# Two loads of a state-space and MLP kernel change places: the second piece of b1 and the broadcast of b2

## The chip, the cores and the metric

The kernel runs on one core of one Trainium2 chip. The core has TensorE (matmuls into PSUM, 8 banks), VectorE, ScalarE and GpSimd, which compute side by side, and SyncE (SP), which here only issues DMAs. ScalarE can issue DMAs too. The metric is the device time of one execution in microseconds. Before the change it is 149.21 us, the median of 3 runs (149.14 to 149.53).

## What is computed

The input x has 2048 rows of 448 columns (bf16). A layer norm gives xn. One branch is a diagonal state-space layer over the 2048 rows, the other a small MLP on a second layer norm of xn; the result is `x + s * silu(mlp)`:

```python
def reference(x, ..., w1, b1, w2, b2):            # cut to what matters
    xn = layernorm(x)
    # state space: 448 complex states, one recurrence over the rows
    Bu = xn @ B_bar.T                              # B_bar from Lambda, dt, B
    h[t] = Lam_bar * h[t - 1] + Bu[t]
    s = 2 * (h @ C.T).real + xn * Dskip
    # MLP, 448 -> 1792 -> 448
    y = layernorm(xn)
    g = gelu_tanh(y @ w1 + b1) @ w2 + b2
    return x + s * silu(g)
```

b1 has 1792 values, b2 has 448. Both are small; what matters here is when they arrive and what their loads stand in front of.

## The kernel before

**Groups.** The rows are worked in four groups of 512 rows (`NG = 4`), each of two blocks. Per group: both layer norms, the transposes of the normalized rows, the matmuls with B (`bu`, line 657), the recurrence as scans on VectorE (`ssm`, line 681), the first MLP layer (`mm1`, line 723), the second (`mm2`, line 748), and the output matmuls with C (`ym`, line 768).

**The order is written out by hand.** Every step is a task with the keys that it reads and writes; `emit` (line 131) walks the list `ORDER` (line 206), and each engine gets its tasks in that order. An engine runs its list strictly in order: where a task waits, all that stands behind it on that engine waits too. A number in `ORDER` is the place of a task among those without a name, in the order in which the program makes them; a name (`H000`, `T1`, `U03`) is a named TensorE task. The PSUM bank of every result is written out as well (`BANKS`); a task that takes over a bank waits for all tasks that used it before.

The numbers that matter here:

- 11 to 13: the loads of x, blocks 0 and 1 (lines 387 to 389); 37: x of blocks 2 and 3 (line 405)
- 14, 15: the two halves (k = 0, 1) of the first chunk of w1; 21 to 26: the halves of chunks 1, 2 and 3 (`ldw1`, line 382). All go through SP's queue.
- 16 to 18, then 19 and 20: loads that ScalarE issues. 19 is the first piece of b1 (two of its 14 columns of 128, line 393), 20 the second (the other twelve, line 394): 128 partitions with three runs of 4 values each, so 384 runs of 8 bytes.
- 35: b2 copied to all 128 partitions (`b2bc`, line 403), 128 times the same 896 bytes, on SP's queue. Its first reader is the head of `mm2` (line 754), which puts b2 into the PSUM banks of the second layer.
- 38: `b1f`, b1 from bf16 to f32, on ScalarE (line 527). It needs both pieces of b1. Every GELU uses it as its bias.
- 78, 83, 88: ScalarE's copies of the transposed first group out of PSUM (line 458).
- 96, 100, ...: the GELUs of the first layer (line 741 for half tiles, line 729 for whole ones).

**The first group.** Its first three pairs of w1's columns are done in two halves of rows (`mm1_half`, line 733: `H000`, `H010`, `H020`, `H011`, ...), so that work can begin when the first blocks are there. Each half pair takes two PSUM banks, so four of them fill all eight; the next one needs a GELU to have drained its banks. Before `H000` TensorE runs matmuls on a tile of zeros (line 809), which compute nothing.

**What else the steps of the prediction touch.** The cosines and sines of the recurrence are made once (`tables`, line 588): VectorE's steps at lines 591 to 596, then the sine on ScalarE (line 602), behind a table load (line 348) that follows the last GELU of the first group, and VectorE's negative copy of it (line 604). VectorE's list has the statistics of the second group's rows (line 430) ahead of these steps. The matrix B comes by transposing DMAs on SP (line 399); VectorE copies its last columns (line 626) and clears a part (line 627) before `bu` can use them at line 668.

Of the kernel before, what the change touches and what calls it, by code (L numbers as in the profile page):

```python
# [203 lines left out]


ORDER = [int(k) if k.isdigit() else k for k in """
18 17 16 4 11 12 13 14 2 3 ST I0 I4 0 35 10 1 I1 I2 I6 74 75 76 19 79 80 81 77 84 82 85 7 15 89 90 T0 78 I5 86 21 T2 I3 87 20 9 91 94 92 83
I7 H000 PV T1 39 6 41 8 40 88 T3 42 93 117 38 22 23 H010 95 44 H020 99 H011 103 96 H021 100 101 24 25 26 37 224 222 226 34 144 228 31 H04 32
104 102 105 223 118 5 54 55 H05 109 45 43 33 123 47 106 122 H001 227 115 225 229 46 111 48 110 112 124 314 49 230 97 H06 98 H03 113 193 107
56 121 125 198 DH 28 202 30 50 53 52 63 116 60 126 127 129 114 108 131 128 132 134 58 59 61 64 65 120 199 200 119 27 203 318 312 316 234 235  # L210
206 204 207 311 315 241 237 205 231 57 62 67 69 130 232 36 313 317 29 70 194 208 195 209 196 135 238 136 145 166 197 236 137 233 U00 167 66
# [670 lines left out]
```

## Time and profile before

| | before |
|---|---|
| median of 3 runs | 149.21 us |
| the profiled execution | 149.81 us |
| its span, first to last instruction | 147.8 us |
| TensorE busy, share of the span | 141.7 us, 96% |
| VectorE | 128.1 us, 87% |
| ScalarE | 103.6 us, 70% |
| GpSimd | 42.0 us, 28% |
| moved by DMA | 14.08 MB |

The profile is one execution. Its times count from the start of the span. "PE" is TensorE, "PEld" its weight loads, "DVE" VectorE, "ACT" ScalarE, "POOL" GpSimd, and a q behind an engine's name is its instruction queue, where DMAs are issued; L741 is line 741 of the program. A row of the timeline gives start, length, engine, line, operation, what it writes and reads, its size and how many instructions are merged in it; in square brackets stands how long the engine was idle before and what ended that. The chain that ended last is followed back from the last instruction, at each step to what released it. "To landing" is the time from the issue of a DMA until all of it has arrived.

### The profile page before, as it was taken

The page shows a single profiled execution, that of the slowest core. Times are in us where ns is not written, and L with a number is a line of the kernel's source. Part 1 is how long each engine was busy: PE and PEld are TensorE (multiplying, and loading weights), DVE is VectorE, ACT ScalarE, POOL GpSimd, SP SyncE. Part 2 cuts the span into 40 slices and gives each one's busy share as a digit, 9 for nine tenths or more (in the row PEclk, how much of TensorE's full clock was granted, in tenths as well). Part 3 has the DMA queues.
Part 4 walks back from the last instruction along what each step waited for, and adds up shares of the span by engine and source line. Part 5 has one row for each costly group of instructions (what it writes and reads, how often), then busy time and mean ns, then how long its engine had stood idle before and what let it go on. Part 6 is the DMA issues. An engine that isn't in the chain of part 4 may idle for free.

```text
span 147.8 us, 2863 instructions
## 1 busy us (share of the span) xinstructions
PE 141.7 (96%) x1092; PEld 72.8 (49%) x1092; DVE 128.1 (87%) x182; ACT 103.6 (70%) x148; POOL 42.0 (28%) x88
## 2 busy tenths in 40 slices
PE   6984999999999999999999999999999999999993
PEld 1573644554454434555553544554435455555563
DVE  2942992597499999989999998999999999999994
ACT  3225999989989989999988999924996610090300
POOL 2589397630000499760000005000009500000000
PEclk9999999999999999999999999999999999999999
DMA  4699997699793300100254601035003300003033
GB/s 105 187 352 347 368 178 146 108 244 155 127 161 61 75 0 4 36 0 18 45 114 103 122 1 42 0 59 101 4 0 98 98 0 7 0 0 98 0 124 124
DMA packets 32083, 14.08 MB, mean 95 GB/s; under 512 B 24131, under 2 KB 31686, under 8 KB 32070
## 3 DMA queue, kind: packets, MB, share of 16 engines
q1 hardware_dynamic: 31376, 13.83, 40.7%
q8 instruction: 8, 0.13, 0.4%
q10 hardware_dynamic: 694, 0.07, 0.4%
q14 instruction: 5, 0.04, 0.1%
HBM read 5.63 MB, written 1.84 MB: 50 GB/s over the span
## 4 chain that ended last, share of the span: by engine, by line
PE 91%; DMA 4%; DVE 2%; ACT 1%; issue 0%; ACTq 0%
PE psum L648 40%; PE psum L762 29%; PE psum L780 14%; DMA b1b<-in_B_b_dram 4%; PE psum L809 3%; PE psum L668 2%; PE psum L783 2%; PE psum L754 1%; DVE t L786 1%; DVE tmp L790 1%; ACT gT L741 1%; PE psum L455 0%; ACT b1f L527 0%; DVE still L339 0%; ACTq L158 0%
## 5 line engine op out<-in xcount | busy, mean ns | idle before, releaser
L648 PE MATMUL psum<-xn2T,w_sb 64*128 64x512 bf16 (+1 forms) x434 | 44.9, 356 | 2.5 <-ACT gT L741 2.1
L762 PE MATMUL psum<-w_sb,gT 128*128 128x448 bf16 x224 | 43.7, 353 | 0.0
L729 ACT ACTIVATE gT<-psum,b1f 128x512 bf16<-128x512 f32 x50 | 30.8, 696 | 5.6 <-PE psum L648 5.6
L648 PEld LDWEIGHTS psum<-xn2T,w_sb 64*128 64x128 bf16 x434 | 23.3, 108 | 21.8 <-ACT gT L741 2.3
L762 PEld LDWEIGHTS psum<-w_sb,gT 128*128 128x128 bf16 x224 | 21.7, 98 | 21.3 <-issue 1.3
L692 DVE TENSOR_TENSOR_SCAN s_f<-cw,cur,v_sb 128x512 f32<-128x512 f32 x21 | 25.8, 1268 | 0.1
L780 PE MATMUL psum<-CQ,h_sb 128*128 128x448 bf16 (+2 forms) x119 | 24.8, 342 | 0.0
L648 PE MATMUL psum<-xnT,BT 64*128 64x512 bf16 x168 | 20.1, 376 | 0.0
L705 POOL TENSOR_TENSOR cwk<-s_f,ang 128x8 f32<-128x8 f32 x3 | 4.3, 1419 | 44.4 <-ACT s_f L702 44.4
L498 ACT ACTIVATE xn_sb<-x_all,lnw 128x512 bf16<-128x512 bf16 x21 | 16.7, 814 | 0.1
L696 ACT ACTIVATE s_b<-s_f 128x3072 bf16<-128x3072 f32 x4 | 11.0, 2760 | 7.2 <-DVE s_f L692 7.2
L780 PEld LDWEIGHTS psum<-CQ,h_sb 128*128 128x128 bf16 x119 | 10.9, 98 | 7.4 <-issue 0.4
L766 ACT ACTIVATE g_sb<-psum 128x448 bf16<-128x448 f32 x16 | 8.2, 537 | 9.1 <-PE psum L762 8.9
L648 PEld LDWEIGHTS psum<-xnT,BT 64*128 64x128 bf16 x168 | 7.9, 94 | 10.4 <-issue 1.5
L665 ACT ACTIVATE u_sb<-psum 128x1024 bf16<-128x1024 f32 x10 | 10.2, 1022 | 0.6 <-PE psum L648 0.6
L430 DVE BATCH_NORM_STATS2 lnst<-x_all 128x6 f32<-128x448 bf16 x12 | 7.1, 608 | 3.3 <-DMA x_all<-in_A_x_dram 3.3
L786 DVE TENSOR_TENSOR t<-psum,g_sb 128x448 bf16<-128x448 f32 (+2 forms) x17 | 9.6, 584 | 0.1
L692 DVE TENSOR_TENSOR_SCAN s_f<-cw,v_sb 128x512 f32<-128x512 f32 x7 | 8.1, 1201 | 0.0
L809 PE MATMUL psum<-still 128*128 128x128 bf16 (+1 forms) x30 | 6.5, 353 | 1.2 <-DVE still L339 1.0
L477 POOL TENSOR_SCALAR lnw<-lnmv 128x4 f32<-128x4 f32 x2 | 1.4, 675 | 20.4 <-DVE lnmv L434 20.4
L714 DVE TENSOR_TENSOR h_sb<-pa,pb 128x3072 bf16<-128x3072 bf16 x4 | 7.0, 1754 | 0.1
L685 DVE TENSOR_TENSOR pb<-u_sb,WT 128x3072 bf16<-128x3072 bf16 x4 | 7.0, 1753 | 0.1
(118 smaller groups left out, 164.7 us busy)
## 6 DMA issues: line engine op xcount, KB each, us to landing
out_dram<-tmp SPq DMA_DIRECT2D x7, 224.0 KB, 2.3
w_sb<-in_B_w_dram SPq DMA_DIRECT2D x6, 256.0 KB, 5.5
x_all<-in_A_x_dram SPq DMA_DIRECT2D x3, 448.0 KB, 7.1
w_sb<-in_B_w_dram SPq DMA_DIRECT2D x3, 448.0 KB, 9.2
u_sb<-u_sb SPq DMA_DIRECT2D x8, 64.0 KB, 1.9
s_b<-s_b SPq DMA_DIRECT2D x8, 64.0 KB, 1.9
w_sb<-in_B_w_dram SPq DMA_DIRECT2D x2, 128.0 KB, 3.7
x_all<-in_A_x_dram SPq DMA_DIRECT2D x2, 112.0 KB, 2.1
```

The source lines that it names most:

```text
L430: dve([lambda e, b=b, r=r, q=q: e.bn_stats(lnst[:, q, :], x_all[:, xa(2 * g + b, r), :])], [f"x{2 * g + b}"], [f"st{q}"], 0.61)
L498: ("act", lambda e: e.activation(dst, src, ACT.Identity, bias=nb, scale=rs), 0.81)]
L648: return lambda e: e.matmul(out(k), wt(k, d, halves[h]), rhs(k, d, halves[h]), start=first and d == 0, stop=not first and d == 3)
L665: kb.either(("act", lambda e: e.activation(u_sb[:, i, :, :], psum[:, bank.b:bank.b + 2, :], ACT.Copy), 1.02), ("dve", lambda e: e.tensor_c ...
L692: dve(lambda e, i=i, ri=ri, init=init: e.tensor_tensor_scan(s_f[:, i, ri, :], col(R1, i).to_broadcast([128, NK]), v_sb[:, i, ri, :], init, ...
L696: act(lambda e: e.activation(s_b[:, 0:3, :, :], s_f[:, 0:3, :, :], ACT.Copy), SF, ["sb"], 2.76)
L729: act([lambda e, k=k: e.activation(gT[:, gb, 2 * j + k, :], psum[:, bank.b + k, :], ACT.Gelu_apprx_tanh, bias=b1f[:, 2 * j + k:2 * j + k + ...
L762: fns = [lambda e, fi=fi, bk=bk, q=q: e.matmul(psum[:, bk.b, 0:D], gT[:, gb, fi, q * 128:(q + 1) * 128], w2_sb[:, fi, :], start=False, sto ...
L766: act(lambda e, gs=gs, bk=bk: e.activation(g_sb[:, gs, :], psum[:, bk.b, 0:D], ACT.Silu), [bk.key] + (["silu"] if g == 0 else []), [f"g{gs ...
L780: fns = [lambda e, k=k: e.matmul(psum[:, bank.b, c0:c1], h_sb[:, hb, k, k0:k0 + 128], CQ[:, k, c0:c1], start=(k == 0), stop=(k == 6)) for ...
L786: dve(lambda e: e.tensor_tensor(t3[:, ob, r, c0:c1], psum[:, bank.b, c0:c1], g_sb[:, gs, c0:c1], ALU.mult), [bank.key, f"g{gs}"], [f"t3{ob ...
L809: pe([lambda e, idle=idle, c=c: e.matmul(psum[:, idle.b, 0:c * 128], still[:, :], still[:, None, :].to_broadcast([128, c, 128]), start=Tru ...
```

## The change

Only the list `ORDER` is changed. Task 20, the second load of b1, moves on ScalarE's queue from behind the first copy of transposed rows (78) to right behind the first load of b1 (19). Task 35, the broadcast of b2, moves on SP's queue from between the halves of w1's first chunk (14 and 15) to behind the last half of w1's last chunk (26) and ahead of the x load of blocks 2 and 3 (37). The same DMAs are issued, by the same engines, with the same sizes; all compute tasks keep their order.

```diff
 ORDER = [int(k) if k.isdigit() else k for k in """
-18 17 16 4 11 12 13 14 2 3 ST I0 I4 0 35 10 1 I1 I2 I6 74 75 76 19 79 80 81 77 84 82 85 7 15 89 90 T0 78 I5 86 21 T2 I3 87 20 9 91 94 92 83
-I7 H000 PV T1 39 6 41 8 40 88 T3 42 93 117 38 22 23 H010 95 44 H020 99 H011 103 96 H021 100 101 24 25 26 37 224 222 226 34 144 228 31 H04 32
+18 17 16 4 11 12 13 14 2 3 ST I0 I4 0 10 1 I1 I2 I6 74 75 76 19 20 79 80 81 77 84 82 85 7 15 89 90 T0 78 I5 86 21 T2 I3 87 9 91 94 92 83 I7
+H000 PV T1 39 6 41 8 40 88 T3 42 93 117 38 22 23 H010 95 44 H020 99 H011 103 96 H021 100 101 24 25 26 35 37 224 222 226 34 144 228 31 H04 32
```

## The prediction

> **What bounds the kernel now.** I read the page first, for the chain of work that ended last.
>
> ```profile
> span 147.8 us, 2863 instructions
> ...
> PE 91%; DMA 4%; DVE 2%; ACT 1%; issue 0%; ACTq 0%
> ```
>
> TensorE is 91% of the chain; what is not TensorE is 4% of a DMA. The chain in order of time says which DMA, and when:
>
> ```profile
> 6.50 6.26 DMA b1b<-in_B_b_dram
> 12.84 0.22 ACT b1f L527
> 13.09 0.85 ACT gT L741 x2
> ```
>
> Columns are start, length, what. Only once does the chain leave TensorE between its first matmul and the tail: the second load of b1 is issued at 6.50, lands at 12.76, ScalarE converts b1 (L527), does the first GELU (L741), and then TensorE goes on. Two waits of VectorE, which I need below for what has room, are in the wait view (total, times, longest):
>
> ```profile
> DVE WT L604 <- ACT WT L602: 4.2, 1, 4.2
> ...
> DVE u_sb L666 <- PE psum L648: 2.6, 1, 2.6
> ```
>
> The timeline of the first 25 us holds the rest (start, length, engine, what):
>
> ```profile
> 1.95 0.36 ACTq L107 DMA_DIRECT2D b1b<-in_B_b_dram  x1
> 2.19 0.47 SPq L107 DMA_DIRECT2D w_sb<-in_B_w_dram  x1
> 2.71 0.47 SPq L107 DMA_DIRECT2D b2bc<-in_B_b_dram  x1
> ...
> 3.21 3.51 SPq L107 DMA_DIRECT2D w_sb<-in_B_w_dram  x7
> ...
> 6.49 0.60 ACT L458 ACTIVATE xn2T<-psum 128x512 bf16<-128x512 bf16 x1 [3.29 <-PE psum L455]
> ...
> 6.98 0.59 ACT L458 ACTIVATE xn2T<-psum 128x512 bf16<-128x512 bf16 x1
> ...
> 9.10 0.60 ACT L458 ACTIVATE xn2T<-psum 128x512 bf16<-128x512 bf16 x1
> ...
> 9.44 2.48 PE L648 MATMUL psum<-xn2T,w_sb 64*128 64x256 bf16 x42
> ...
> 13.90 1.15 DVE L430 BATCH_NORM_STATS2 lnst<-x_all 128x6 f32<-128x448 bf16 x2 [3.34 <-DMA x_all<-in_A_x_dram]
> ...
> 20.36 2.74 DVE L596 SCALAR_TENSOR_TENSOR s_f<-pb,cw,s_f 128x512 f32<-128x512 f32 x4
> ...
> 21.36 0.37 PE L754 MATMUL psum<-b2bc,mean 32*128 32x448 bf16 x4
> ...
> 24.02 1.28 ACT L348 ACT_TABLE_LOAD   x1
> ```
>
> The 42 matmuls from 9.44 fill the last free pair of PSUM banks and stop: ScalarE can't drain a bank without b1f. TensorE alone, in two windows:
>
> ```profile
> 7.85 0.61 PE L648 MATMUL psum<-xn2T,w_sb 64*128 64x256 bf16 x8 [0.25 <-DMA w_sb<-in_B_w_dram]
> ...
> 8.67 0.62 PE L455 MATMUL psum<-ident,xn_sb 128*128 128x128 bf16 x8
> ```
> ```profile
> 13.98 0.41 PE L648 MATMUL psum<-xn2T,w_sb 64*128 64x256 bf16 x4 [2.06 <-ACT gT L741]
> ```
>
> So two idle gaps stand in this stretch: 0.25 us for the second half of w1's first chunk, 2.06 us for b1.
>
> **The change part by part.** The loads, with the time from issue to landing (last column, the median; rows of the DMA view over 2.0 to 6.9 us, where the x2 are the two halves of w1's chunk 0):
>
> ```profile
> w_sb<-in_B_w_dram SPq DMA_DIRECT2D x2, 128.0 KB, 3.7
> b2bc<-in_B_b_dram SPq DMA_DIRECT2D x1, 112.0 KB, 4.3
> b1b<-in_B_b_dram ACTq DMA_DIRECT2D x1, 0.5 KB, 2.9
> b1b<-in_B_b_dram ACTq DMA_DIRECT2D x1, 3.0 KB, 6.3
> ```
>
> *b1's second load.* It is issued at 1.95 + 0.36 = 2.31 instead of 6.50. The first load of b1, issued just ahead of that, took 2.9 us. The later one took 6.3 because it stood behind seven w1 loads: the last of them, issued around 6.2, took 6.4 us by its own row:
>
> ```profile
> DMA to landing us min/median/max: 6.4/6.4/6.4
> ```
>
> It landed at 12.6 to 12.7, the b1 load at 12.76: the order of issue, over both queues. At 2.31 the queues hold x and one small piece of w1, so I expect a landing between 2.31 + 2.9 = 5.2 and 2.31 + 6.3 = 8.6, and take 5.5 (nearest: the neighbour issued 0.36 us before it). The Trainium skill, page "DMA: Bandwidth & Descriptors", section "Queues, rings and completion order", says that each DMA engine takes turns between the queues, packet by packet. By it the load did not stand behind SP's loads, its 6.3 us are its own, and it would land at 8.6; the landing right behind the last w1 load speaks against it, and the gain would be the same, with less room.
>
> ScalarE can't use b1f sooner anyway: L527 stands in its order behind the copy of 9.10, which ends at 9.70. Then 0.22 for b1f, and the first GELU when its half tile is done, 14 of the 42 matmuls after 9.44, about 10.4; at 0.85 it ends near 11.3. TensorE asks for that bank at 11.92. So the 2.06 us go entirely, with some 0.6 us of room; and the landing may be as late as about 10.3. The moved issue, about 0.4 us of ScalarE's queue as the one before it, costs nothing: ScalarE waits until 6.49, 3.29 us long, for TensorE's first transposes. Where it stood it is over before the copy of 6.98, so at most nothing is gained there either.
>
> *Its 384 small pieces (128 partitions x 3, 8 bytes each) ahead of w1.* The DMA rate in windows of 2 us (last column, GB/s):
>
> ```profile
> 4.50:6.50 2.00, 1.94 (x14) 1.17 (x12) 1.90 (x8) 0.01 (x1) 0.90 (x3) 1.00 0.45 108
> 8.50:10.50 2.00, 1.85 (x33) 1.67 (x33) 0.91 (x3) 0.78 (x2) 1.75 (x5) 1.00 1.10 380
> 10.50:12.50 2.00, 1.42 (x27) 1.16 (x22) 0.06 (x1) 0.00 (x0) 1.75 (x6) 1.00 1.18 313
> ```
>
> In 10.5 to 12.5, shortly before b1 lands, the rate is 313 for 380: (380 - 313) x 2 us = 134 KB, or 0.35 us for whatever stands behind it. That is now w1.
>
> *b2's broadcast leaves w1.* In 4.5 to 6.5, while b2's copy is under way (2.71 + 4.3 = 7.0), the DMAs move 108 GB/s, though seven w1 loads are being issued. I put this slow stage down to the broadcast. Without it the second half of chunk 0, issued at 2.71 instead of 3.21, lands between 5.7 and 7.65. Before, it landed just ahead of the matmul of 7.85, at 7.8, 4.6 after its issue; by the median of 3.7 the first half took 2.8 and landed at 5.0. The early end is 5.0, 128 KB at 380 GB/s, and 0.35 for b1; the late end is 7.8, 0.5 earlier and 0.35 later. TensorE needs it when the copy of 6.98 ends, 7.57. Gain on the 0.25 gap: 0.2, bounds 0.15 and 0.25. The next matmuls, at 9.44, wait for chunk 1, issued at 4.20 and 5.1 us under way, so landed at 9.3:
>
> ```profile
> DMA to landing us min/median/max: 5.1/5.1/5.1
> ```
>
> The transposes from 8.67 end at 9.29. An earlier landing is worth 0 to 0.2; I take 0.1, because the second group of transposes still waits for VectorE. Head together: 0.3, bounds 0.15 and 0.45.
>
> *b2's broadcast behind w1.* Its reader, L754, starts at 21.36. Issued at 6.3, with even 6.4 us it is there at 12.7: no cost. Next on SP is the x load of blocks 2 and 3, whose landing at 13.9 starts VectorE's run from 13.90. In both orders the same bytes stand ahead of it, so I take no change. Bounds: 1.4 later, if the slow stage was not the broadcast's and comes once more, 2 us x (1 - 108/380); 1.4 earlier, if the stage is now hidden.
>
> *What takes over.* TensorE would be 2.06 + 0.3 = 2.4 us early. What does not move with it? VectorE's work behind the x load runs until 20.36 + 2.74 = 23.10, and the sine (L602) needs it. Rows of 25 to 75 us:
>
> ```profile
> 24.93 2.25 SPq L106 DMA_TRANSPOSE BT<-in_A_B_im_dram  x1
> ...
> 25.40 1.91 ACT L602 ACTIVATE WT<-s_f 128x2048 bf16<-128x2048 f32 x1
> ...
> 31.09 0.28 DVE L626 COPY BT<-BT 128x512 bf16<-128x512 bf16 x1
> ...
> 31.65 0.11 DVE L627 MEMSET BT<- 64x64 uint32 x1
> ...
> 33.03 1.03 PE L668 MATMUL psum<-xnT,BT 128*128 128x512 bf16 x4
> ...
> 33.24 0.54 ACT L766 ACTIVATE g_sb<-psum 128x448 bf16<-128x448 f32 x1 [0.46 <-PE psum L762]
> ...
> 34.10 0.60 ACT L670 ACTIVATE u_sb<-psum 128x512 bf16<-128x512 f32 x1 [0.32 <-PE psum L668]
> ```
>
> Now the sine starts at 25.40, behind the table load of 24.02. With the GELUs 2.4 earlier that load ends at 22.9, and the sine waits for VectorE until 23.2: 2.2 us early. ScalarE waits for TensorE at 33.24 and 34.10, 0.78 us in all, and takes up the missing 0.2 there. VectorE has 2.6 us of waiting at L666. Then L668, TensorE's first matmul of the recurrence: it comes at 33.03 and needs the memset that ends at 31.76, slack 1.27. If nothing ahead of that memset moved, the gain would stop at 1.27. But VectorE's wait of 4.2 us for the sine (L604) moves with the sine, and of what the memset needs the last B transpose is issued at 24.93 and takes 5.2, so it is there at 30.1 at the latest:
>
> ```profile
> DMA to landing us min/median/max: 5.2/5.2/5.2
> ```
>
> From the copy's start to the memset's end it is 31.76 - 31.09 = 0.7, so 30.8 for a TensorE that arrives at 33.03 - 2.4 = 30.6: a loss of 0.2 at most, and I take 0.1. Behind this point all engines follow TensorE or one another, and the chain shows no other engine until the tail.
>
> **Sum:** 2.06 + 0.3 - 0.1 = 2.3 us (rounded). The profiled execution took 149.81, its span 147.8 and 2.0 around it: it should become 147.5, with a span of 145.5. The median of the three runs is 149.21, 0.6 below; by the same gain 146.9.
>
> **Rivals.** *The gain is cut at L668.* The transposes and VectorE's list don't follow, and the 1.27 us of slack is all there is: 149.21 - 1.27 = 147.9. For it: the transposes share a loaded DMA queue. Against it: the landing of 30.1 even unmoved.
>
> *The stall only moves: no change, 149.2.* The change doesn't do what it says: b1 is issued 4.2 us earlier and lands no earlier than 12.8, since its own packets or w1's, now running together, are the slow ones, and TensorE stops at the same bank for the same 2.06. For it: 6.3 us is the only price of this very load in the trace. Against it: even that price gives 8.6; it would have to be 10.5.
>
> *Slower: the broadcast delays x.* The x load sets VectorE's run, that run the sine, the sine ScalarE's list. The gain is used up when x lands 2.2 + 0.78 us late, at 13.9 + 3.0 = 16.9; from there each us costs one. If b2's whole 4.3 us stood in front of x, it would land at 18.2, for 149.21 + 1.3 = 150.5. For it: the 108 GB/s stage, and that VectorE waited 3.34 us for x. Against it: b2 stands ahead of x already.
>
> **How the numbers follow.** Forecast 0.75; cut at L668 0.14; moved stall 0.06; x late 0.05. About 0.3% (0.45 us) is what a measurement of this kernel can tell from no change; both cases of gain lie beyond it: faster 0.89, same 0.06, slower 0.05. The predicted time is the forecast's, 146.9. The forecast's own bounds are gains of 2.06 + 0.15 - 0.2 = 2.0 (with x 1.4 late the sine is 0.8 early instead of 2.2, and with the 0.78 of room the gain is 1.6) and 2.06 + 0.45 = 2.5, plus 0.1 because the 2.06 counts from the modelled end of a matmul: 146.6 at best. The upper end takes in the cut at L668 and the spread of the three runs (0.3): 148.2.
>
> **What would show it.** Right: the second b1 issue at about 2.3, landed before 9; b1f at about 9.7; no wait of TensorE for L741 near 12 to 14; the first w1 matmul at about 7.6; the sine at about 23.2, behind VectorE and not behind the table load; L668 at about 30.7; the chain without b1b. Wrong: a new TensorE wait at L668 over 0.5 us, x landing after 14.7, or b1 landing beyond 10.3.

## The result, and the profile after

| | before | after |
|---|---|---|
| median of 6 runs of each, on one chip | 149.50 us | 147.62 us |
| lowest to highest | 149.14 to 149.71 | 147.25 to 148.31 |
| the profiled execution | 149.81 us | 148.12 us |
| its span | 147.8 us | 146.1 us |

The changed kernel is faster: the ratio of the means is 0.9884, with a 95% interval of 0.9856 to 0.9913. That is 1.7 us (149.5 x 0.0116), between 1.3 and 2.2. The forecast was 2.3, so the mechanism is to be checked and the missing part to be found. Some executions of any of these kernels run over 1.5% above its fastest, some of them with a granted clock of 0.989; the medians and ratios below leave these out.

The chain of waits of the changed kernel, in order of time (start, length, what):

```profile
9.13 9.67 PE psum L648 x126
18.80 0.30 PE psum L754 x4
19.10 0.77 PE psum L648 x6
19.87 10.70 PE psum L762 x56
30.57 0.84 issue
31.41 1.02 PE psum L668 x4
32.43 20.61 PE psum L648 x190
```

The DMA of b1 has left the chain. 126 matmuls of the first layer run without a break where 42 had run before the stop. A new piece stands at 30.57: TensorE is idle for 0.84 us and then starts L668, the first matmul with B. "issue" names nobody. The timeline of the same kernel does (start, length, engine, what; idle time before it in brackets):

```profile
1.94 0.84 ACTq L107 DMA_DIRECT2D b1b<-in_B_b_dram  x2
2.19 4.07 SPq L107 DMA_DIRECT2D w_sb<-in_B_w_dram  x8
...
5.29 0.38 PE L455 MATMUL psum<-ident,xn_sb 128*128 128x128 bf16 x4
...
6.30 0.47 SPq L107 DMA_DIRECT2D b2bc<-in_B_b_dram  x1
...
7.33 0.61 PE L648 MATMUL psum<-xn2T,w_sb 64*128 64x256 bf16 x8
...
9.08 0.21 ACT L527 ACTIVATE b1f<-b1b 128x14 f32<-128x14 bf16 x1
...
22.99 1.91 ACT L602 ACTIVATE WT<-s_f 128x2048 bf16<-128x2048 f32 x1 [0.30 <-DVE s_f L596]
23.46 1.49 SPq L107 DMA_DIRECT2D Dbc<-in_A_Dskip_dram  x1
...
25.00 1.21 SPq L106 DMA_TRANSPOSE BT<-in_A_B_im_dram  x1
...
30.63 0.30 DVE L626 COPY BT<-BT 128x512 bf16<-128x512 bf16 x1 [0.78 <-DMA BT<-in_A_B_im_dram]
31.19 0.11 DVE L627 MEMSET BT<- 64x64 uint32 x1
31.41 0.81 PE L668 MATMUL psum<-xnT,BT 128*128 128x512 bf16 x3 [0.84 <-issue]
```

The reader is to follow the last four rows backwards. L668 starts 0.11 after the memset ends (31.30); VectorE reached the copy ahead of it 0.78 early and waited for the last B transpose, which was issued at 25.00 and landed at 30.60. The DMA view of that stretch gives the last two transfers (operation, KB, time from issue to landing):

```profile
Dbc<-in_A_Dskip_dram SPq DMA_DIRECT2D x1, 112.0 KB, 6.1
...
BT<-in_A_B_im_dram SPq DMA_TRANSPOSE x1, 5.6
```

The same view of before:

```profile
Dbc<-in_A_Dskip_dram SPq DMA_DIRECT2D x1, 112.0 KB, 4.8
...
BT<-in_A_B_im_dram SPq DMA_TRANSPOSE x1, 5.2
```

Dskip is copied to all 128 partitions as b2 is, and stands directly ahead of that transpose on SP's queue. Before, it was issued at 24.30 (0.58 us) and the transpose at 24.93; now at 23.46, but its issue takes 1.49, so the transpose is no earlier at all (25.00), and lands 0.5 later (30.08 to 30.60).

How much this costs is best read from start to start. From the first matmul of L762 to that of L668 there are 10.60 us before (22.43 to 33.03) and 11.61 after (19.80 to 31.41): 1.0 us is lost. Up to L762 TensorE had gained 22.43 - 19.80 = 2.63; at L668 1.62 is left, and the span is 1.7 shorter.

### The profile page after: what moved, and what is told of

It is laid out like the page before. It is cut to its first block, busy times and chain, and to the rows that moved or that the text cites. A ratio compares the mean times of both kernels' runs of the same rounds, so it can differ in the third digit from the quotient of the medians.

```text
span 146.1 us, 2863 instructions
## 1 busy us (share of the span) xinstructions
PE 141.0 (97%) x1092; PEld 72.7 (50%) x1092; DVE 128.3 (88%) x182; ACT 103.6 (71%) x148; POOL 42.5 (29%) x88
## 4 chain that ended last, share of the span: by engine, by line
PE 91%; DVE 5%; DMA 1%; issue 1%; POOL 0%; DVEq 0%
PE psum L648 42%; PE psum L762 29%; PE psum L780 14%; PE psum L668 3%; PE psum L783 2%; DVE lnst L446 2%; DMA x_all<-in_A_x_dram 1%; DVE t L786 1%; PE psum L754 1%; DVE xn_sb L451 1%; DVE tmp L790 1%; DVE lnmv L447 0%; POOL lnw L450 0%; DVE lnw L448 0%; PE psum L455 0%
## 5 line engine op out<-in xcount | busy, mean ns | idle before, releaser
L762 PE MATMUL psum<-w_sb,gT 128*128 128x448 bf16 x224 | 43.7, 353 | 0.0
L762 PEld LDWEIGHTS psum<-w_sb,gT 128*128 128x128 bf16 x224 | 21.7, 98 | 21.3 <-issue 1.3
L780 PE MATMUL psum<-CQ,h_sb 128*128 128x448 bf16 (+2 forms) x119 | 24.9, 342 | 0.0
L696 ACT ACTIVATE s_b<-s_f 128x3072 bf16<-128x3072 f32 x4 | 11.1, 2764 | 7.2 <-DVE s_f L692 7.2
L780 PEld LDWEIGHTS psum<-CQ,h_sb 128*128 128x128 bf16 x119 | 10.9, 98 | 7.4 <-issue 0.4
L684 DVE TENSOR_TENSOR pa<-u_sb,WT 128x3072 bf16<-128x3072 bf16 x4 | 7.0, 1750 | 0.1
```

The costliest lines, as they stand in the source:

```text
L684: dve(lambda e: e.tensor_tensor(pa[:], wide(u_sb, 0), WT[:, 0:3, 1:3, :], ALU.mult), U + WK, ["pa"], 1.76)
L696: act(lambda e: e.activation(s_b[:, 0:3, :, :], s_f[:, 0:3, :, :], ACT.Copy), SF, ["sb"], 2.76)
L762: fns = [lambda e, fi=fi, bk=bk, q=q: e.matmul(psum[:, bk.b, 0:D], gT[:, gb, fi, q * 128:(q + 1) * 128], w2_sb[:, fi, :], start=False, sto ...
L780: fns = [lambda e, k=k: e.matmul(psum[:, bank.b, c0:c1], h_sb[:, hb, k, k0:k0 + 128], CQ[:, k, c0:c1], start=(k == 0), stop=(k == 6)) for ...
```

## The experiments

Two theories stood at the start. **A:** the gain is b1's load alone; b2's move is worth little, and what is missing is lost at L668, where Dskip's copy holds up the last B transpose. **B:** b2's move is a part of the gain, or of the loss.

### One part alone: e1 and e2

e1 moves only task 20, e2 only task 35, both in the list of before.

```diff
-76 19 79
+76 19 20 79
-87 20 9
+87 9
```
```diff
-0 35 10
+0 10
-26 37
+26 35 37
```

> Only b1's second load is moved; b2's broadcast stays between the halves of w1's first chunk. Theory A (the stall of 2.06 us was b1's landing alone, and what caps the gain is the last transposed quarter of B at L668): no wait for L741 near 12 us, the first second-layer matmul (L762) about 2.2 us earlier than before (22.43), L668 at 31.3 to 31.6 as in the changed kernel, time 147.5 to 147.9. Theory B (b2's leaving w1 gives a good part of the gain, or b1's small pieces ahead of w1 slow it while the broadcast stands there too): first w1 matmul later than 7.9, L762 less than 1.8 us early, time 148.2 or more.

> Only b2's broadcast is moved behind w1; b1's second load is issued at 6.5 as before. Theory A (loads of both queues are served in the order of issue): b1 lands right behind the last w1 load, which is now at 11.0, so at 11.1 to 11.5 instead of 12.76, the stall for L741 shrinks from 2.06 to 0.3 to 0.8, time 147.9 to 148.5. Theory B (queues take turns, b1's 6.3 us are its own): b1 lands at 12.5 to 12.8 again, stall 1.9 to 2.1, time 149.2 to 149.6.

e1 ran 147.55 us, where before ran 149.58, ratio 0.987 (0.9828 to 0.9912): all that the whole change brings. Its chain has no DMA in this stretch, and the same 126 matmuls in one piece:

```profile
9.12 9.67 PE psum L648 x126
...
30.56 0.16 issue
30.72 1.02 PE psum L668 x4
```

So the first part of A's expectation for e1 came (L762 2.64 earlier, at 19.79), and the second did not: L668 was expected at 31.3 to 31.6. e2 ran 149.98, ratio 1.0012 (0.9984 to 1.0041): nothing. In e2 TensorE still stops; its row, and then the chain:

```profile
14.10 0.30 PE L648 MATMUL psum<-xn2T,w_sb 64*128 64x256 bf16 x2 [2.28 <-ACT gT L741]
```
```profile
6.39 6.48 DMA b1b<-in_B_b_dram
```

The A recorded for e2 had expected b1 to land at 11.1 to 11.5, a stall of 0.3 to 0.8 and 147.9 to 148.5 us, with the broadcast no longer ahead of b1; all three were missed. That was a misreading of the order: the broadcast is now issued at 6.29, just ahead of b1's 6.39, and the two land at 12.50 and 12.87. The numbers of e2's B (12.5 to 12.8, a stall of 1.9 to 2.1, 149.2 to 149.6) are near, but not for its reason: the 6.3 us are not the load's own, since the same load issued early takes 3.1, as e1 and the changed kernel show (2.31 to 5.39; 2.33 to 5.41). Of the two theories at the start, the times bear out that the gain is b1's load alone. Whether b2's move adds to the loss at L668 stays open: L762 to L668 takes 0.32 longer than before in e1's one profile, and 0.64 to 1.20 longer in the three of the changed kernel, but the times are alike.

### Dskip's copy behind the last B transpose: e3, and again as e9

```diff
-232 36 313 317 29 70 194
+232 313 317 29 36 194
-323 239
+323 70 239
```

Task 36 is the copy of Dskip, 29 the last B transpose, 70 the first reader of Dskip (L585), which has to move along. The edit stands on the changed kernel.

> The changed kernel with the broadcast of Dskip (36) moved behind the last transposed quarter of B (29), and its first reader on VectorE (70) moved behind 323, ahead of the evacuation at L666. Theory A (the broadcast of Dskip holds up that quarter of B and so L668): B lands at 27 to 28.5 instead of 30.6, the wait of TensorE at L668 (0.84) goes, L668 at 30.4 to 30.7, span 145.0 to 145.5, time 146.6 to 147.0. Theory B (the transposes are slow by themselves or the cap is VectorE's list): B lands after 29.8, L668 within 0.2 of 31.4, time 147.4 to 147.8.

> The changed kernel with the broadcast of Dskip behind the last quarter of B, once more, one look. Theory A: B lands before 28.5 again, no wait at L668, L668 within 0.2 of 30.4. Theory B (the first profile of it was a lucky one): a wait of 0.3 or more at L668.

The transposing load is issued at 22.66 in e3 and lands at 26.80 instead of 30.60. L668 waits for nothing (timeline of e3):

```profile
30.35 1.03 PE L668 MATMUL psum<-xnT,BT 128*128 128x512 bf16 x4
```

In e9 it lands at 28.16 and L668 starts at 30.52, without a wait too, as A expected. L762 to L668 is 10.61 us in both profiles, as before the change. So the place of the loss is shown. The moved reader (L585) is not what helps: in the changed kernel its wait for Dskip ends at 29.62, 0.98 before B lands. The time is not shown: e3 ran 147.81, ratio 0.9881 (0.9841 to 0.9921), like the changed kernel, where 146.6 to 147.0 was expected. The profile of e3 is its fastest execution (span 145.1, 1.0 less than the changed kernel's). That of e9 has a span of 146.3, and shows where half of these 1.2 us went; its waits from 30 to 67 us (total, times, longest):

```profile
DVE xn_sb L497 <- DMA xn2T<-xn_sb: 2.2, 1, 2.2
...
PE psum L648 <- DMA xnT<-xn_sb: 0.4, 1, 0.4
```

Dskip's copy now stands ahead of the x load and the xn2T transposes; in e9 it lands at 31.15, VectorE waits 2.2 us for xn2T, and TensorE stops at 45.47 and 65.31 for 0.4 and 0.2. In e3 it lands at 28.91, and TensorE stops nowhere behind it. So what stands behind this copy can be late; moving the copy chooses who that is.

### The same bytes from distinct rows: e4 and e5

In e4 (on before) b2's place is filled from 128 different rows of w2, and in e5 (on the changed kernel) Dskip's too. 112 KB each, the same operations; the values of b2, and in e5 of Dskip, are not the reference's.

```diff
-            ld("sp", b2bc[:], dram_ap(B_b2, 0, [[0, 128], [1, D]]), ["b2bc"], 114688)
-            ld("sp", Dbc[:], dram_ap(A_Dskip, 0, [[0, 128], [1, D]]), ["Dbc"], 114688)
+            ld("sp", b2bc[:], dram_ap(B_w2, 0, [[D, 128], [1, D]]), ["b2bc"], 114688)
+            ld("sp", Dbc[:], dram_ap(B_w2, 128 * D, [[D, 128], [1, D]]), ["Dbc"], 114688)
```

> The kernel before, with b2's copy read from 128 different rows of w2 (same sizes, wrong b2) instead of 128 times from the same 896 bytes. Theory A (reading the same 896 bytes over and over is what makes 4.5 to 6.5 us slow): the DMA rate there is over 250 GB/s instead of 108, the second half of w1's first chunk lands before 6.3 instead of 7.8, the second load of b1 before 11.7, and the time falls to 147.7 to 148.6. Theory B (the slow stretch belongs to the start of the queues and not to the broadcast): rate 100 to 130 there, landings within 0.3 us of before, time 149.2 to 149.6.

> The changed kernel with both copies (b2's and Dskip's) read from 128 different rows of w2 each, same sizes and places (b2 and Dskip are wrong). Theory A (128 reads of the same 896 bytes are what makes these two loads slow, and Dskip's is what holds up the last quarter of B): Dskip's load lands in under 4 us instead of 5 to 6, the last quarter of B before 29.3, no wait at L668 above 0.2, x of blocks 2 and 3 before 13.2, span 145.0 to 145.5. Theory B (the transposes around it are slow, not the repeated read): landings within 0.5 us of the changed kernel's and a wait at L668 of 0.4 or more.

The window from 4.5 to 6.5 us in e4 (last column, GB/s):

```profile
4.50:6.50 2.00, 1.77 (x19) 1.11 (x18) 1.93 (x8) 0.57 (x1) 0.80 (x4) 1.00 0.89 230
```

230 GB/s where before had 108, with the order of before. In e1 the broadcast is still there and the window has 171; in the ten profiles from which it is gone the window has 198 to 286. So the repeated reads of the same 896 bytes slow this stretch, by how much differs from execution to execution. For the time that is worth little: b1 lands at 11.85 instead of 12.76 and the stall is 1.54 instead of 2.06; 149.10 us, ratio 0.9954 (0.9924 to 0.9984). The direction was A's, but its numbers were all missed: 230 for over 250 GB/s, the second half of w1's first chunk at 6.86 for 6.3, b1 at 11.85 for 11.7, and the time of 147.7 to 148.6, since b1 was still issued behind w1 loads.

e5 ran 147.3, ratio 0.9848 (0.9813 to 0.9884), with spans of 145.1 to 145.4 and no wait at L668; its DMA view:

```profile
Dbc<-in_B_w_dram SPq DMA_DIRECT2D x1, 112.0 KB, 4.4
...
BT<-in_A_B_im_dram SPq DMA_TRANSPOSE x1, 4.5
```

The issue of the copy takes 0.58 us instead of 1.49, the transpose behind it is issued at 23.11 and lands at 27.62. The order on the queue is the changed kernel's; only the sources differ. This speaks for the repeated source, and against the 112 KB or the place, but does not prove it. SP reaches the copy 0.98 earlier here (22.48), b2's source was changed as well, and the copy's own 4.4 us miss the expected "under 4": with the repeated source, in other places, it took 4.2 in e3 and in e6. x landed at 13.43, where under 13.2 was expected.

### How steady the wait at L668 is: e7 and e8, the changed kernel again

> The changed kernel once more, for a second profile and for times on the same chip as the others here. Theory A: the wait at L668 differs from execution to execution with the landing of the last quarter of B (30.6 in the first profile, wait 0.84): with a landing at 30.0 or earlier the wait is under 0.3 and the span 145.3 to 145.6. Theory B (the wait is a fixed price of the change): 0.7 to 1.0 again, span 146.0 to 146.2.

> The changed kernel a third time, one look: as for the second, span minus the wait at L668 should be 145.2 to 145.3 under theory A whatever the wait is; under theory B the wait is 0.7 to 1.0.

The rows of e7 and of e8:

```profile
31.03 1.02 PE L668 MATMUL psum<-xnT,BT 128*128 128x512 bf16 x4 [0.48 <-issue]
```
```profile
32.01 0.81 PE L668 MATMUL psum<-xnT,BT 128*128 128x512 bf16 x3 [1.04 <-issue]
```

With the first profile that is 0.84, 0.48 and 1.04; e1 has 0.16. The last B transpose landed at 30.60, 30.13, 31.15 and 29.82. So the wait is there in all three profiles of the changed kernel, but its size moves by half a microsecond. e7 ran 147.81, ratio 0.9883 (0.9845 to 0.992); e8, one execution, 149.0. Of e7's profiled execution only the trace is read here: it took 149.81 us for the same span of 146.1, so the rest lies outside the span.

That the wait accounts for the whole spread was A's expectation, and it was missed: the span less the wait should have been 145.2 to 145.3, and is 145.2, 145.6 and 145.9. B's fixed price of 0.7 to 1.0 was missed as well. In e8, 0.40 of the rest is the head (L762 at 20.20 for 19.80). And there is a second place: at its first L780 (67.13 before, 65.32 in e7, 66.31 in e8) TensorE's lead over before falls once more, from 2.00 to 1.81 in e7 and from 1.02 to 0.82 in e8. The chain of e8 comes there from VectorE:

```profile
65.24 0.68 DVE CQ L621
65.92 0.35 DVE h_sb L716
66.31 0.36 PE psum L780
```

### The B transposes ahead of Dskip's copy and of more: e6, again as e11, and with b2 behind x: e10

```diff
-28 202 30 50
+28 202 30 27 29 50
-119 27 203
+119 203
-232 36 313 317 29 70 194
+232 36 313 317 194
-323 239
+323 70 239
```

e10 is this and moves b2's broadcast behind the x load of blocks 2 and 3 as well:

```diff
-26 35 37 224 222 226 34 144
+26 37 224 222 226 34 35 144
```

> The changed kernel with the two late quarters of B (27 and 29) issued right behind the early ones, ahead of the transposes of the normalized rows (120 and 119), and the first reader of the broadcast of Dskip (70) moved behind 323. Theory A (what is left of the forecast's 2.3 us is lost at L668 in some executions, by the landing of the last quarter of B behind the broadcast of Dskip): B lands before 26, both row transposes before 28, no wait at L668, L668 at 30.3 to 30.5, span 145.0 to 145.3 in nearly every execution, time 0.3 to 0.6 below the changed kernel. Theory B (the spread of the changed kernel's times comes from elsewhere): the times spread over 1 us as before, and the median is within 0.2 of the changed kernel's.

> The kernel with B first (e6) once more, one look. Theory A (only the landing of the late quarter of B is lost time behind the first layer; the rest of the spread is when TensorE's clock comes up in the first 8 us): no wait at L668, and L668 earlier by the same amount as L762, 2.2 to 2.7 us against the kernel before. Theory B: a wait at L668 over 0.3 again.

> The kernel with B first (e6), and b2's copy moved on, behind the x load of blocks 2 and 3 and one load of w2. Theory A (the order of the loads is the order of landing): x lands 1.2 to 1.5 us earlier, at 12.3 to 12.8, b2 at 14.5 to 15.5, well ahead of its reader; the sine no longer waits for VectorE; TensorE is not bound there, so the time is that of e6 within 0.3, 147.3 to 147.9. Theory B (VectorE's start holds the kernel as well): 0.4 us or more below e6.

The last B transpose lands at 25.34, 25.12 and 25.94, and L668 waits in none of the three; the rows of e6 and of e10:

```profile
30.76 1.03 PE L668 MATMUL psum<-xnT,BT 128*128 128x512 bf16 x4
```
```profile
30.40 1.03 PE L668 MATMUL psum<-xnT,BT 128*128 128x512 bf16 x4
```

e6 ran 147.61 (147.54 to 147.98), ratio 0.9868 (0.9824 to 0.9912); e11, one execution, 147.48; e10 147.22, ratio 0.9864 (0.9822 to 0.9905), and x landed at 12.59 in it instead of 13.74. These are the lowest ratios apart from e5's, 2.0 us (149.63 x 0.0136) for e10, but their intervals overlap the changed kernel's, and e1's 0.987 is hardly above them. On the same chip e6 is 0.2 below e7's 147.81, where A had 0.3 to 0.6 and B within 0.2; e6's six times lie closer together than the changed kernel's, as A had it. e10 is 0.4 below e6, just between its two theories. That these orders beat the changed kernel is likely by the profiles and not shown by the times.

## Why the prediction was right, and where it was not

**The number.** 147.62 lies in the stated range of 146.6 to 148.2, 0.7 above the forecast of 146.9; 0.3 of that is the reference, whose median is 149.50 over six runs and was 149.21 over three. The rest comes from one term of the sum, L668 below: 1.0 us of loss where 0.1 was taken, less a lead before it of 2.63 where 2.4 was taken. The mechanism that gives the gain is the one that was forecast.

**b1's load: right.** Issue at 2.31 and landing at 5.5 were forecast; 2.33 and 5.41 came. The first GELU stood at 10.12 for 10.4. The stall went entirely, and e1 shows that this alone is the gain. It was worth a little more than the 2.06 in its bracket: from the matmul of H010 to L762 there were 12.99 us (9.44 to 22.43), now 10.73 (9.07 to 19.80), so 2.26. Issued early the load takes 3.1 us, so half of the 6.3 was the price of being issued behind w1; the landings follow the order of issue over both queues in before (12.62, 12.76), e2 (12.50, 12.87, 13.85) and e4 (10.99, 11.85, 12.06). The moved stall, a rival, is refuted by the same numbers. Less sure is how that price comes about. The Trainium skill ("DMA: Bandwidth & Descriptors", "Queues, rings and completion order") says that a DMA engine takes turns between the queues. That does not make the 6.3 us the load's own, as the prediction read it, because a load that takes turns with w1 is slowed by w1. The traces have something of both: in e4, where the load is issued at 5.94, the queue of b1's pieces moves 1 packet until 8 us, then 265 from 8 to 10 and 134 from 10 to 12, beside 744, 578 and 757 on the queue of SP's loads. So it starts late, and then runs side by side with w1.

**The head: the sum right by luck.** 0.3 was forecast for b2's broadcast leaving w1, and H010 came 0.37 earlier (9.07). But e1, with the broadcast in its old place, has 9.05, e2, with it moved, 9.34, and e8, which is the changed kernel, 9.46. So the broadcast's place is not what sets H010. In e1 the second half of w1's first chunk lands at 7.03, behind the broadcast, and TensorE does not wait for it; so the 0.25 us of waiting before, with the landing at 7.80, are not the price of that place by itself. In the changed kernel and in e2 TensorE waits for VectorE instead (at L455, 0.5 and 0.2 us in all). And TensorE's own pace varies: the four transposes at L455 take 0.60 us before,

```profile
5.85 0.60 PE L455 MATMUL psum<-ident,xn_sb 128*128 128x128 bf16 x4
```

and 0.38 after (the row at 5.29 in the timeline above). The 0.35 for b1's small pieces ahead of w1 was not seen, and not measured by itself.

**The broadcast behind w1: right, no cost.** The slow stretch was the broadcast's, as forecast (e1, e2, e4), if not always as slow as 108 GB/s. It comes once more behind w1: the last w1 load lands at 11.01, b2 at 12.39, 1.4 later. Since the same bytes stood ahead of x in both orders, x lands at 13.74 for the forecast 13.9. The rival in which x is late is refuted. Nor does the move bring anything (e2).

**The sine: right.** 22.99, 0.30 behind VectorE, for 23.2 behind VectorE.

**L668: the term that was mis-sized.** The prediction put the loss at "0.2 at most", because the last B transpose was "there at 30.1 at the latest". It measured 1.0 start to start (0.84 in the bracket), and 0.64 and 1.20 in e7 and e8 (19.78 to 31.03 and 20.20 to 32.01, less 10.61). The step that failed is the words "at the latest". It took for granted that a transpose in the same place of the queue needs no more than its 5.2 us and is issued no later; it landed at 30.60, which is 0.5 of the 1.0. The DMA directly ahead of it moved 0.84 earlier and took 6.1 instead of 4.8, its issue 1.49 instead of 0.58; e3 and e6 take that copy out of the way, e5 changes its source, and in each the wait is gone. But the landing is not all: in e7 it is 30.13, as the bound has it, and 0.64 is lost all the same. In the first profile and in e7 TensorE was 2.63 and 2.65 early at L762 and not 2.4, and the sum left out what lies between landing and copy and between memset and L668, 0.14 and 0.22 us (30.60 to 30.63 and 31.30 to 31.41; 30.13 to 30.25 and 30.93 to 31.03). The rival "the gain is cut at L668" thus holds in part: B did not follow, and 1.62 of the gain is left where the rival had 1.27 and the forecast 2.3. Its price might have been found by asking of the transpose's neighbour on SP's queue what had been asked of b2: both are the same kind of copy. That behind L668 all engines follow TensorE held in the first profile of the changed kernel, and not quite in e7 and e8 (0.2 at L780).

With the measured terms the sum is 2.26 + 0.37 - 1.01 = 1.62, against a span that is 1.7 shorter. The wrong sign that the prediction named for itself, a new wait at L668 over 0.5 us, is the one that came.

**What stays open.** Why Dskip's copy takes 4.2 to 6.1 us from one execution to the next, and whether that is its source alone; what makes repeated reads slow; whether b2's move has a part in the loss at L668; and whether e10 is faster than the changed kernel.

## What to carry to other kernels

A small load that is issued behind large ones can land behind them, as b1's did: before costing it by its own issue-to-landing time, compare its landing with that of its neighbours in issue order. When a stall is removed, the next due time must be checked for each transfer that it needs together with the transfer just ahead in its queue; "it is there by then even if nothing moves" is no bound while that neighbour moves. And undo a two-part change by parts: here one part was all of the gain.

## What the runs showed of the hardware

- A copy that reads the same 896 bytes 128 times was slower than one of the same size from distinct rows. Behind the last w1 load b2 landed 1.38 us later (11.01 to 12.39) in the changed kernel, 0.80 to 1.77 in the eight profiles with this order and the repeated source, and 0.31 (11.77 to 12.08) in e5. What stood behind such a copy was held up with it. From 27 to 29 us the x load is queued behind Dskip in both the changed kernel and e5; in the first the copy is under way until 29.60, and 65 GB/s are moved, in e5 it has landed at 26.87, and 289 are moved; first the window of the changed kernel, then of e5:

```profile
27.00:29.00 2.00, 2.00 (x12) 1.08 (x11) 1.61 (x6) 2.00 (x4) 1.53 (x7) 1.00 0.85 65
```
```profile
27.00:29.00 2.00, 2.00 (x12) 1.05 (x11) 1.97 (x9) 2.00 (x3) 1.59 (x7) 1.00 1.11 289
```

- The same four transposes took 0.38 to 0.60 us in the first 6 us, though the granted clock (the column ahead of the DMA share) stays at 1.00. The Trainium skill, page "TensorE: Matmul & The Clock Gate", "Part 1: The HAM clock gate", says that TensorE starts at half its clock until it has been busy for some 3.4 us, with a scatter of half a microsecond between runs. The spread fits that in size; no run here shows the gate itself.
